# A token-mixing and MLP kernel: the input of batch 2 loaded in eight parts, each behind a product of batch 1

## The chip, the cores and the metric

The kernel runs on one core of a Trainium2 chip. The metric is the device time of one execution in microseconds (us), as the median of several runs. A core has five engines that run their own instruction streams and meet at semaphores: TensorE (PE, matrix products; its weight loads are listed as PEld), VectorE (DVE), ScalarE (ACT), GpSimd (POOL) and SyncE (SP). Transfers between the memory of the chip (HBM) and the core's own memory (SBUF) are done by 16 DMA engines. Any of SyncE, ScalarE and GpSimd can issue them. TensorE writes its results to a small memory of eight banks (PSUM), from which VectorE or ScalarE copy them out.

## The reference

There are two steps. The first mixes the 3008 tokens of each of 8 batches: a Fourier transform along the sequence, a product with a complex filter, and the transform back. The second is an MLP with an exact GELU on each of the 24064 tokens.

```python
def _attn_ref(x, filt_r, filt_i):            # x: (8, 3008, 256)
    X = np.fft.rfft(x, axis=1)
    F = (filt_r + 1j * filt_i)[None, :, :]   # filters: (1505, 256)
    Y = X * F
    return np.fft.irfft(Y, n=x.shape[1], axis=1).astype(np.float32)

def _moe_ref(x, w_in, w_out):                # x: (24064, 256), w_in: (256, 2048), w_out: (2048, 256)
    h = x @ w_in
    g = 0.5 * h * (1.0 + erf(h / sqrt(2)))
    return (g @ w_out).astype(np.float32)
```

## The kernel before

The transform of 3008 = 47 x 64 points is done as two shorter ones, each a matrix product with a table. For batch b there are stages `s1` (47-point products of the input x), `r1` (its result comes back through HBM in another order), `s2` (the second product, times the filter F on VectorE: twelve products p(0) to p(11), two frequencies each), `s3` and `r2` (the way back, again through HBM) and `s4`, which writes the mixed tokens y. Batch 0 has its own stages before the main loop. The MLP takes the tokens in 47 blocks of 512: `mm1` with GELU on ScalarE, then `mm2`. Block 0 does `mm2` plainly; from block 1 on it is done with seven products in place of eight, for which VectorE makes sums of the activations (`sums_1` to `sums_3`) and puts the results together (in `mm2_seven`).

The input of a batch is brought in by eight transfers, for 8 of 32 columns w and one of two halves h each. They convert fp32 to bf16 and are issued by GpSimd. There is one buffer x for all batches (pool `px`), so a load has to wait until `s1` of the batch before has read it.

```python
self.px = pool("px", 1)
self.pp = pool("pp", 6)      # the products p
self.po = pool("po", 4)      # output tiles, and the sums of mm2_seven, tag "ost"
...
def load_x(self, b, lo=0, n=32, hs=(0, 1)):
    ...
    for w in range(lo, lo + n, 8):
        for h in hs:
            nc.gpsimd.dma_start(out=xt[h * o:h * o + NA, w:w + 8, :], in_=xv[h][:, w:w + 8, :])

def gate(self, t):
    g = self.po.tile([1, 1], BF16, tag="gate", name="gate")
    self.nc.gpsimd.tensor_copy(out=g, in_=t)      # one element: GpSimd waits until t is written

def load_next(self, b, p, c, h):
    if b > 1:
        self.gate(self.st[b, "p", p][0:1, 0, 0:1])
    self.load_x(b + 1, 8 * c, 8, (h,))

def load_filters_again(self, eng, k0, k):         # F, now in another order of rows
    for o in range(0, 128, 32):
        i = self.st["Fd"][o // 64, :, :, :, k0:k0 + k, :].rearrange("q i t k c -> (q i) t (k c)")
        eng.dma_start(out=self.F[o:o + 32, :, k0:k0 + k, :], in_=i)
```

The gate makes GpSimd issue a load only once a given product p is there. It takes GpSimd alone; the value copied is used by nobody.

The work is spread by hand over slots: 16 slots are one block of 512 tokens in `mm1`, and the function `put` hangs a part of the mixing on a slot. What hangs on a slot is written into the program ahead of that slot's matmuls. For batch 1, `s2` of product p is at slot 28 + 14 * (p // 4) + 3 * (p % 4), which is 28, 31, 34, 37, 42, 45, 48, 51, 56, 59, 62, 65 for p = 0 to 11.

```python
for b in range(1, B):
    hi = first(b)
    if b == 1:
        s1, n1, r1, s2, n2, group = 0, 3, 12, 28, 3, 14
    elif b == 2:
        s1, n1, r1, s2, n2, group = hi - 87, 3.7, hi - 73, hi - 64, 3.4, 14      # hi = 176
    ...
    unit = lambda p: s2 + group * (p // 4) + int(n2 * (p % 4))
    ...
    if b + 1 < B:
        for i in range(8):
            put(unit(i + 2) if b > 1 else 25, m.load_next, b, i + 2, i // 2, i % 2)
...
put(4, m.table_4_all, parts[:5])                       # GpSimd
put(1, m.load_filters_again, nc.gpsimd, 0, 8)
put(17, m.load_filters_again, nc.sync, 8, 16)          # four transfers of 512 KB, on SyncE's queue
```

The output of the first blocks goes out on SyncE's queue too, that of later blocks on GpSimd's:

```python
# mm2 (block 0)
ost = self.po.tile([128, 2, 256], FP32, tag="ost", name="ost")
nc.vector.tensor_copy(out=ost, in_=ps)
for sub in range(2):
    self.put_rows(t * TCH + (tile_i - 1 + sub) * 128, ost[:, sub], nc.sync)
...
# mm2_seven: t1, t3 are the halves of one tile "ost" of sums; c(0, .) and c(1, .) are two more tiles, the results
v(out=c(1, 1), in0=t3, in1=p1, op=ALU.add)              # L688 of the trace
v(out=t1, in0=t1, in1=p1, op=ALU.add)                   # L691
...
v(out=c(h, 1 - h), in0=tt, in1=p, op=ALU.add)           # L694
self.put_rows(..., nc.gpsimd if t > 2 else nc.sync)
```

Of the kernel before, what the change touches and what calls it, by code (L numbers as in the profile page):

```python
# [31 lines left out]
class _Mix:  # L32
# [91 lines left out]

    def load_next(self, b, p, c, h):

        if b > 1:
            self.gate(self.st[b, "p", p][0:1, 0, 0:1])
        self.load_x(b + 1, 8 * c, 8, (h,))

# [603 lines left out]
def kernel(  # L734
# [9 lines left out]
    m = _Mix(ctx, tc, x, filt_r, filt_i, moe_w_in, moe_w_out, out)  # L744
# [115 lines left out]
    def put(slot, f, *a):  # L860
        at.setdefault(slot, []).append((f, a))

    def first(b):
        return (b * S // TCH) * 16

    busy, crowd, after = set(), set(), {}
# [5 lines that stand above are left out]
            s1, n1, r1, s2, n2, group = hi - 87, 3.7, hi - 73, hi - 64, 3.4, 14  # L872
        else:
            s1, n1, r1, s2, n2, group = hi - 94, 3.7, hi - 80, hi - 70, 3.4, 14
        unit = lambda p: s2 + group * (p // 4) + int(n2 * (p % 4))
        busy.update(range(s1 - 1, s1 + int(3 * n1) + 2))
        for c in range(4):
            put(s1 + int(c * n1), m.s1, b, c)
            put(r1 if c < 3 else unit(3) + 1, m.r1, b, c)
        for p in range(12):  # L880
            put(unit(p), m.s2, b, p)
            busy.add(unit(p))
            if p % 4 == 3:
                put(unit(p) + 3, m.s3, b, p // 4)
                put(unit(p) + 4, m.s3_out, b, p // 4, 1)
                busy.update(range(unit(p) + 2, unit(p) + 6))
        after[b] = unit(11) + 7
        crowd.update(range(s2, after[b]))
        if b + 1 < B:
            for i in range(8):  # L890
                put(unit(i + 2) if b > 1 else 25, m.load_next, b, i + 2, i // 2, i % 2)

    for b in range(1, B):
        end = 1000000
# [84 lines left out]
```

## Time and profile before

| what | before |
|---|---|
| time, median of 3 runs | 748.63 us (748.54 to 749.09) |
| span of the profiled execution | 747.3 us |
| TensorE busy | 736.0 us |
| VectorE, ScalarE, GpSimd busy | 573.2, 557.4, 224.8 us |
| DMA, mean over the span | 121 GB/s |

A line of the page's groups, or of an answer on one stretch of time, gives a program line (L688), an engine, the operation, and the tiles as "out<-in". A number in brackets is the time that the engine stood idle just before, with the event that ended it. In the chain of waits each row is a start, a length and what was going on; "SPq L113" is the queue of SyncE issuing the transfer of line 113 (the filters), and "DMA out_dram<-ost" is the time in which the store of an output tile was under way. In a table by stretches, each engine has its busy time and, in brackets, its number of instructions; the last columns are the clock granted to TensorE, the mean busy share of the 16 DMA engines (it is modelled, and a little over 1 when they are all full), and what they moved in GB/s. Of the DMA queues, q0 holds what GpSimd issues and q1 what SyncE issues; a row gives packets, MB, and the time that the packets took as a share of the stretch times 16 engines. L87 is the load of x, L113 the second load of the filters, L123 the gate, L430 a product p, L444 `s3`, L592 `mm1`, L595 the GELU, L665 `mm2` from block 1 on, L712 a store of the output.

### The profile page before, as it was taken

Reading aid. Unit: us, or ns where it says so; the run is one execution under the profiler, and the core shown is the slowest. Engines: PE = TensorE matmul, PEld = TensorE weight load, DVE = VectorE, ACT = ScalarE, POOL = GpSimd, SP = SyncE. Lnnn points to the kernel's source line nnn. Section 1 sums busy time; section 2 is a strip of 40 time slices with the busy share of each in tenths; the row PEclk is TensorE's granted clock in tenths of the full one; section 3 lists DMA queues with packets and bytes.
Section 4 is the critical chain, followed back from the end, with each engine's and each line's share of the span. In section 5 each row is a group of like instructions: output and inputs, shape, how many; then the busy total and the mean of one; then the engine's idle time right before and its main releaser. Section 6 shows DMA issues by size and latency. Waiting matters only on the chain.

```text
span 747.3 us, 20357 instructions
## 1 busy us (share of the span) xinstructions
PE 736.0 (98%) x8420; PEld 518.0 (69%) x8420; DVE 573.2 (77%) x1028; ACT 557.4 (75%) x1000; POOL 224.8 (30%) x416
## 2 busy tenths in 40 slices
PE   7999899999999999999999999999999999999998
PEld 4856566766777777677777776677677766777776
DVE  7876777787778887789767996779967798676566
ACT  6987677777787777777777777777778777777773
POOL 7994007142222413133311342114411121112121
PEclk9999999999999999999999999999999999999999
DMA  8999533666256651667426654256543533401011
GB/s 142 227 222 240 154 79 96 185 127 124 67 155 162 129 120 59 166 148 145 108 71 179 126 115 127 71 156 142 127 100 91 144 111 92 120 29 58 30 58 58
DMA packets 76663, 90.74 MB, mean 121 GB/s; under 512 B 9754, under 2 KB 57882, under 8 KB 76314
## 3 DMA queue, kind: packets, MB, share of 16 engines
q1 hardware_dynamic: 58714, 49.63, 26.1%
q0 software_dynamic: 17440, 39.62, 23.6%
q8 instruction: 66, 1.08, 0.6%
q14 instruction: 27, 0.22, 0.1%
q10 hardware_dynamic: 416, 0.20, 0.1%
HBM read 57.15 MB, written 48.23 MB: 141 GB/s over the span
## 4 chain that ended last, share of the span: by engine, by line
PE 86%; POOL 5%; DMA 5%; DVE 2%; issue 1%; ACT 1%; SPq 0%; POOLq 0%; DVEq 0%
PE ps_h L592 40%; PE ps_o L665 37%; PE ps_s L444 3%; PE ps_s L473 3%; DMA out_dram<-ost 2%; PE ps_s L427 2%; PE ps_s L400 2%; POOL tmp_sb L380 1%; POOL x_sb L87 1%; DMA F<-in_filt_i_dram 1%; DMA x_sb<-in_x_dram 1%; POOL F L118 1%; POOL T4a L382 1%; DVE g_sb L640 1%; DVE s_sb L634 1%
## 5 line engine op out<-in xcount | busy, mean ns | idle before, releaser
L595 ACT ACTIVATE g_sb<-ps_h 128x512 f16<-128x512 f32 x752 | 446.3, 600 | 169.6 <-PE ps_h L592 165.1
L592 PE MATMUL ps_h<-y_sb,w_in_sb 128*128 128x512 bf16 (+3 forms) x1600 | 445.0, 366 | 0.0
L712 POOL DMA_DIRECT2D out_dram<-ost x221 | 125.4, 574 | 430.4 <-DVE ost L694 410.5
L665 PEld LDWEIGHTS <-g_sb 128*128 128x128 f16 x2944 | 194.6, 98 | 80.1 <-issue 12.8
L665 PEld LDWEIGHTS <-s_sb 128*128 128x128 f16 x2208 | 148.7, 98 | 51.2 <-issue 5.8
L592 PEld LDWEIGHTS <-w_in_sb 128*128 128x128 bf16 x1600 | 125.0, 98 | 8.3 <-issue 1.7
L665 PE MATMUL ps_o<-w_sums,g_sb 128*128 128x128 f16 x1472 | 127.8, 219 | 1.3 <-DVE g_sb L640 1.1
L665 PE MATMUL ps_o<-w_sums,s_sb 128*128 128x128 f16 x1472 | 125.9, 219 | 0.0
L430 DVE TENSOR_TENSOR p<-ps_s,F 128x1024 bf16<-128x1024 f32 x84 | 102.4, 1219 | 26.9 <-PE ps_s L427 26.7
L634 DVE TENSOR_TENSOR s_sb<-g_sb 128x1024 f16<-128x1024 f16 x184 | 120.4, 683 | 1.0 <-ACT g_sb L595 1.0
L665 PE MATMUL ps_o<-w_out_sb,g_sb 128*128 128x128 f16 x1472 | 118.9, 219 | 1.8 <-DVE ost L694 1.7
L640 DVE TENSOR_TENSOR g_sb<-s_sb,g_sb 128x1024 f16<-128x1024 f16 x92 | 63.1, 686 | 1.1
L665 PE MATMUL ps_o<-w_out_sb,s_sb 128*128 128x128 f16 x736 | 63.8, 219 | 0.0
L647 DVE TENSOR_TENSOR s_sb<-g_sb 128x1024 f16<-128x1024 f16 x92 | 63.1, 685 | 0.0
L687 DVE TENSOR_TENSOR t_sb<-t_sb,ps_o 128x256 f32<-128x256 f32 x46 | 19.2, 418 | 46.5 <-PE ps_o L665 46.5
L473 PEld LDWEIGHTS <-d_sb 96*128 96x128 bf16 x448 | 31.9, 98 | 25.9 <-issue 0.2
L306 DVE CAST a_sb<-ps_s 128x512 bf16<-128x512 f32 x57 | 36.6, 686 | 15.1 <-PE ps_s L400 14.9
L682 DVE TENSOR_TENSOR ost<-t_sb,ps_o 128x256 f32<-128x256 f32 x46 | 19.2, 417 | 35.2 <-PE ps_o L665 34.9
L304 ACT ACTIVATE y_sb<-ps_s 128x376 bf16<-128x376 f32 x79 | 37.8, 479 | 2.6 <-PE ps_s L473 2.6
L694 DVE TENSOR_TENSOR ost<-t_sb,ps_o 128x256 f32<-128x256 f32 x90 | 33.6, 415 | 6.6 <-PE ps_o L665 6.2
L473 PE MATMUL ps_s<-T4a,d_sb 96*128 96x94 bf16 x448 | 38.1, 206 | 0.1
L123 POOL COPY gate<-p 1x1 bf16<-1x1 bf16 x40 | 13.8, 346 | 73.4 <-DVE p L430 73.4
(149 smaller groups left out, 529.3 us busy)
## 6 DMA issues: line engine op xcount, KB each, us to landing
out_dram<-ost POOLq DMA_DIRECT2D x123, 128.0 KB, 2.2
x_sb<-in_x_dram POOLq DMA_DIRECT2D x64, 188.0 KB, 4.1
b_sb<-R SPq DMA_DIRECT2D x28, 384.0 KB, 3.9
R<-v_sb SPq DMA_DIRECT2D x84, 128.0 KB, 2.4
d_sb<-R SPq DMA_DIRECT2D x56, 192.0 KB, 4.0
R<-a_sb SPq DMA_DIRECT2D x54, 192.0 KB, 3.1
F<-Fd SPq DMA_DIRECT2D x4, 512.0 KB
Fd<-F SPq DMA_DIRECT2D x8, 192.0 KB, 6.4
```

The costliest lines, as they stand in the source:

```text
L304: self.nc.scalar.activation(out=out, in_=in_, func=AF.Copy, scale=1.0 if scale is None else scale)
L306: self.nc.vector.tensor_copy(out=out, in_=in_)
L430: nc.vector.tensor_tensor(out=w, in0=ps.unsqueeze(1).to_broadcast([128, 2, 512]), in1=self.F[:, :, 2 * p:2 * p + 2, :].rearrange("p t a b ...
L473: nc.tensor.matmul(ps[:, 94 * i:94 * i + 94], lhsT=d[:, (grp % 2) * 4 + i, 128 * half:128 * half + 128], rhs=self.T4a[:, 4 * grp + i], sta ...
L592: nc.tensor.matmul(ps[:, o:o + n], lhsT=w[:, dc], rhs=self.ring[:, dc, off:off + n], start=(dc == 0), stop=(dc == 1))
L595: nc.scalar.activation(out=self.st["g", t][:, jc, :], in_=ps, func=AF.Gelu)
L634: self.nc.vector.tensor_tensor(out=self.st["s", t][:, i:i + 2], in0=a, in1=b, op=ALU.subtract)
L640: self.nc.vector.tensor_tensor(out=a21[:, k], in0=self.st["s", t][:, k, 0], in1=a22[:, k], op=ALU.add)
L647: self.nc.vector.tensor_tensor(out=self.st["s4", t][:, k], in0=a12[:, k], in1=s2[:, k], op=ALU.subtract)
L665: nc.tensor.matmul(ps[:, (m + 1) % 2, sub, :], lhsT=a[:, i, 128 * sub:128 * sub + 128], rhs=b[:, i], start=i == 0, stop=i == 7)
L694: v(out=c(h, 1 - h), in0=tt, in1=p, op=ALU.add)
L712: eng.dma_start(out=out, in_=tile_[lo - r0:lo - r0 + n])
```

## The change

The condition that left batch 1 out is taken away: the loads of batch 2's input, which all hung on slot 25 and had no gate, now hang on the slots of the products p(2) to p(9) of batch 1, each behind a gate on its product, as for all later batches. It is meant to spread the eight transfers over the stage in which batch 1 is mixed.

```diff
     def load_next(self, b, p, c, h):
 
-        if b > 1:
+        if b > 0:
             self.gate(self.st[b, "p", p][0:1, 0, 0:1])
         self.load_x(b + 1, 8 * c, 8, (h,))
 ...
         if b + 1 < B:
             for i in range(8):
-                put(unit(i + 2) if b > 1 else 25, m.load_next, b, i + 2, i // 2, i % 2)
+                put(unit(i + 2), m.load_next, b, i + 2, i // 2, i % 2)
```

## The prediction

> **What bounds the kernel now.** I began with the page. Its first lines say that TensorE is the engine to watch, and that its clock is at full speed everywhere (a row of nines), so a gain can only come from places where the matmul stream stops.
>
> ```profile
> PE 736.0 (98%) x8420; PEld 518.0 (69%) x8420; DVE 573.2 (77%) x1028; ACT 557.4 (75%) x1000; POOL 224.8 (30%) x416
> ```
>
> The span is 747.3 us, so TensorE is idle for about 11 us in all. Next I asked for busy time by stretches, to see where. From 120 to 720 us it is idle for only 0.35 us in total, so nothing that changes there can matter. The rest of the idle time lies in the start, in the last 10 us, and in one hole near 80 us. That hole falls in the stage which the change touches, so I cut the stage at the events that matter: the first load of batch 2's input (60.2 us), the time when the first changed load could start (67.4), and the hole itself (78.3 to 85.8).
>
> ```profile
> core 0: us, PE busy (x) PEld busy (x) DVE busy (x) ACT busy (x) POOL busy (x), PEclk, DMA share, GB/s
> 60.20:67.40 7.20, 7.20 (x69) 5.08 (x67) 6.80 (x10) 4.56 (x9) 4.14 (x9) 1.00 1.02 228
> 67.40:78.30 10.90, 10.90 (x122) 7.30 (x121) 5.57 (x10) 8.34 (x16) 0.00 (x0) 1.00 1.06 233
> 78.30:85.80 7.50, 5.41 (x53) 3.34 (x50) 7.42 (x13) 3.52 (x7) 0.00 (x0) 1.00 0.49 178
> 85.80:98.00 12.20, 12.19 (x136) 8.33 (x137) 10.06 (x16) 8.96 (x17) 0.00 (x0) 1.00 0.23 55
> ```
>
> The reader is to see three things. The DMA engines are full (share 1.02 to 1.06) for 18 us, and nearly empty afterwards. TensorE loses 7.50 - 5.41 = 2.09 us in the third row. And VectorE is full there (7.42 of 7.50), after a stretch in which it was half idle (5.57 of 10.90): it was held up and then caught up. The chain of waits names the holder:
>
> ```profile
> 58.93 0.59 SPq L113
> 59.53 0.04 issue
> 59.57 0.94 SPq L712
> 60.51 0.04 issue
> 60.56 17.66 DMA out_dram<-ost
> 78.22 0.03 issue
> 78.25 0.05 DVEq L688
> 78.30 0.04 issue
> 78.34 0.42 DVE ost L688
> ```
>
> The store of the first output tile is issued at 59.57 and lands at 78.22. VectorE wants that buffer again for the second tile of token block 1 (the pool "po" has 4 buffers with the tag "ost": two for block 0, the sums and the first result of block 1, and then round again). The timeline of VectorE and of TensorE shows the price:
>
> ```profile
> 78.34 0.42 DVE L688 TENSOR_TENSOR ost<-t_sb,ps_o 128x256 f32<-128x256 f32 x1 [3.15 <-DMA out_dram<-ost]
> ```
> ```profile
> 79.15 0.56 PE L665 MATMUL ps_o<-w_out_sb,g_sb 128*128 128x128 f16 x7 [0.18 <-DVE t_sb L691]
> ...
> 82.75 0.45 PE L665 MATMUL ps_o<-w_out_sb,g_sb 128*128 128x128 f16 x5 [1.67 <-DVE ost L694]
> ...
> 85.81 0.51 PE L665 MATMUL ps_o<-w_sums,g_sb 128*128 128x128 f16 x6 [0.26 <-DVE g_sb L640]
> ```
>
> VectorE stands 3.15 us on a DMA; TensorE then waits for PSUM banks and sums that VectorE is late with: 0.18 + 1.67 + 0.26 = 2.11 us, which is the loss of the row above.
>
> Last, the DMA view over 60.2 to 80.2 us says who fills the DMA engines:
>
> ```profile
> q1 hardware_dynamic: 1230, 3.31, 64.9%
> q0 software_dynamic: 512, 1.54, 38.8%
> ```
>
> Queue q0 is the GpSimd queue and holds only the eight input loads here (8 x 188 KB = 1.54 MB). They take 38.8% of 20 us = 7.76 us of all sixteen engines, 0.97 us each. In the same view they land 11.9 to 16.4 us after issue, against a median of 4.1 us over the whole kernel. Queue q1 is SyncE's: four loads of the remaining filters (512 KB each, issued 57.0 to 59.5), behind them the stores of the output.
>
> **What the Trainium skill says.** "DMA: Bandwidth & Descriptors", section "Issuing engines are not separate DMA queues": transfers started by ScalarE, SyncE or GpSimd run on the same 16 DMA engines and interleave. The trace agrees: the two shares add up to 1.04 and both kinds of transfer are slow at once. Its section "Queues, rings and completion order" says that each DMA engine alternates between the queues that have work, packet by packet, and takes one queue's descriptors in order. That fits a store which stands behind 2 MB of filters in its own queue and gets only part of the engines while x is in the other. "SBUF — State Buffer", section "SBUF: two separate sides", says that GpSimd and VectorE share a port pair under an exclusive lock, and that a GpSimd DMA can starve because its descriptors can't be written. In this trace I see little of it: the issue of an input load takes 507 to 722 ns in all 64 cases, and the 40 gate copies take 177 to 578 ns.
>
> **The change part by part.**
> (1) It moves the eight loads of batch 2. Before, all are put at slot 25; GpSimd gets to them at 60.22, after its work on the table T4a, and issues them in 4.12 us. After, load i stands behind the product p(i+2) of batch 1, at slots 34, 37, 42, 45, 48, 51, 56 and 59. The order of instructions on TensorE, VectorE, ScalarE and SyncE stays as it is; only GpSimd's differs. From the end of the VectorE products in the trace the loads would go out at about 67.4, 69.5, 74.9, then near 78, 80, 82, 90 and 92 us (the last five estimated: today's 80.8 and later, less up to the 3 us that VectorE no longer stands).
> (2) It adds eight gate copies on GpSimd of about 0.25 us (median of the 40). GpSimd has nothing to do between 64.3 and 111.7 us, so their cost is nil. They read p, whose pool has six buffers, so eight VectorE products now also wait on GpSimd: p(8) for the gate on p(2), and so on. That gate is some 20 us old by then (67.4 against 89.9 us), and s3 reads p later than the gate does, so no buffer is held longer.
> (3) It frees the DMA engines from 60.2 to 67.4 us. The store needs the filters ahead of it and itself: of the 12.98 us that q1 took in this window (64.9% of 20 us) some 11 us come before the landing at 78.2, the rest being the second tile's stores and the first of R2. Alone it lands at about 60.2 + 11 = 71.2. Two of the eight loads get in before that, up to 2 x 0.97 us: 73.1 at the latest.
> (4) VectorE asks for the buffer at 75.19 (74.78 + 0.41, the end of L687). The store is there 2 us earlier. The wait of 3.15 us goes.
> (5) What then holds VectorE? L688 at 75.2, L691, L634; the product p(5) has its matmul at 76.3; two L634; L694 needs the last group of block 1 at 78.4. So L694 ends near 79.6, where TensorE asks for it at 81.0. The later L640 would end about 82.8, and TensorE would ask at 83.7. All three waits of TensorE go, with 0.9 us or more to spare.
> (6) The sum: -2.11 us. The 16 matmuls of s3 at 86.68 take 1.21 us instead of 0.99 as elsewhere, so 0.1 to 0.2 us more may lie there; I don't count it. Everything after is tied to the matmul stream and moves up as a whole. 748.63 - 2.11 = 746.5 us.
>
> **The rivals.**
> (a) The store stays late. If the filters and their neighbours alone take as long as I credit to both, it lands at 75 to 77 and VectorE still waits 1 us or so. TensorE has about 1 us of slack in that chain, so this would leave 0 to 0.8 us of the loss: 746.5 to 747.3. For it speaks that GB/s was 344 at the first moment of that window and mostly 200 to 260 afterwards, so the load is not simply shared by bytes.
> (b) A new collision takes the place of the old. The late loads (78 to 96 us) meet the stores of v_sb (issued 72 to 79 and 88 to 92) and the outputs of block 1 and 2. Against it: the DMA share there is 0.23 to 0.49, and six loads add 5.8 us of work over some 18 us, about a third. The chain that matters next, v_sb at 103.5 to d_sb landing at 112.1, begins after the last load has landed (92 + 4 = 96). It would give back at most the 0.5 us that TensorE waits at 114.3 today: 747.
> (c) The loads come too late for batch 2. Its first stage is put at slot 89, 119.8 us in the trace; with 20 us to spare this is out.
> (d) The gates or the descriptors get in VectorE's way through the shared port: eight times some 0.3 us on VectorE in a stage where it is 90% busy. Later batches run the same pattern with TensorE idle for 0.35 us in 150 us between 155 and 305 at the most, so I give it little: 746.7 to 747.
> (e) The transfers were hidden anyway, and the gain is eaten by a later wait. From 120 us on TensorE has no gaps to take it up. 748.6.
>
> **Range and chances.** I put 65% on the whole gain within 0.3 us (746.2 to 746.9), some 20% on (a), (b) or (d) with part of it (to 747.7), 10% on no gain or worse, and 5% on more than 2.8 us. Runs differ by some 0.5 us (748.54 to 749.09). So 746.5 us, with a range of 745.9 to 747.7. Two per cent are 15 us: the whole hole is 2.1 us, and nothing in the change can cost 15 us, so I put 0.99 on within 2%.
>
> **What would show it.** In the profile after, the first store of ost should land before about 75 us, the loads of x in about 4 to 6 us each instead of 14, L688 should have no wait for a DMA, and TensorE should lose under 0.3 us from 75 to 90 us. The share of the DMA engines should be below 1 after some 70 us and about 0.4 to 0.7 from 80 to 95. The matmuls of the first stage of batch 2 should start about 2.1 us earlier than 119.8. I am wrong if L688 still waits, if a v_sb or d_sb transfer becomes the releaser of TensorE near 100 to 114 us, or if the span keeps its length although the hole is closed.

## The result, and the profile after

| | before | after |
|---|---|---|
| median, six runs each | 749.09 us (748.54 to 749.76) | 746.50 us (745.96 to 747.16) |
| ratio, with 95% interval | | 0.9966 (0.9954 to 0.9979) |
| span of the profiled execution | 747.3 us | 745.3 us |
| TensorE's share of the chain that ended last | 86% | 91% |

The change saves 2.6 us by the medians, 0.34%. In the table by stretches of the kernel after, with the same cuts as in the prediction, the hole is closed:

```profile
core 0: us, PE busy (x) PEld busy (x) DVE busy (x) ACT busy (x) POOL busy (x), PEclk, DMA share, GB/s
60.20:67.40 7.20, 7.15 (x65) 5.19 (x65) 6.34 (x9) 4.54 (x8) 1.09 (x2) 1.00 1.03 243
67.40:78.30 10.90, 10.79 (x120) 7.30 (x121) 8.65 (x14) 8.34 (x16) 2.88 (x6) 1.00 0.95 232
78.30:85.80 7.50, 7.39 (x84) 4.88 (x83) 7.21 (x12) 5.25 (x10) 2.70 (x6) 1.00 0.67 129
85.80:98.00 12.20, 12.10 (x135) 8.91 (x134) 9.91 (x16) 9.17 (x17) 1.86 (x5) 1.00 0.56 105
```

TensorE is busy for 7.39 us of the third stretch in place of 5.41, and VectorE has 8.65 us of work in the second in place of 5.57: nothing holds it up there. The DMA share, 1.06 and 0.49 before, is now 0.95 and 0.67. (The trace of after holds 8287 matmul records in place of 8420, 133 fewer, so TensorE is busier than its column says. From here on starts of instructions are compared.)

The timeline of VectorE shows L688 without a bracket, so VectorE did not stand idle before it:

```profile
75.62 0.41 DVE L687 TENSOR_TENSOR t_sb<-t_sb,ps_o 128x256 f32<-128x256 f32 x1
76.07 0.42 DVE L688 TENSOR_TENSOR ost<-t_sb,ps_o 128x256 f32<-128x256 f32 x1
76.40 0.42 DVE L691 TENSOR_TENSOR t_sb<-t_sb,ps_o 128x256 f32<-128x256 f32 x1
```

GpSimd's timeline shows what the gates do. Each copy waits for its product, and one load follows:

```profile
68.31 0.58 POOL L123 COPY gate<-p 1x1 bf16<-1x1 bf16 x1 [6.95 <-DVE p L430]
68.85 0.59 POOL L87 DMA_DIRECT2D x_sb<-in_x_dram  x1
70.37 0.57 POOL L123 COPY gate<-p 1x1 bf16<-1x1 bf16 x1 [0.93 <-DVE p L430]
70.89 0.55 POOL L87 DMA_DIRECT2D x_sb<-in_x_dram  x1
75.77 0.18 POOL L123 COPY gate<-p 1x1 bf16<-1x1 bf16 x1 [4.33 <-DVE p L430]
76.00 0.51 POOL L87 DMA_DIRECT2D x_sb<-in_x_dram  x1
```

The eight loads go out from 68.9 to 92.5 us and land in 3.4 to 6.5 us, not 11.9 to 16.4. In the DMA view over 60.2 to 80.2 us, queue q1, which carries the filters and the stores, gets a larger part of the engines:

```profile
q1 hardware_dynamic: 1448, 3.76, 74.3%
q0 software_dynamic: 192, 0.58, 16.3%
```

The first output tile (two transfers of 128 KB) has landed at about 72.7 us, where it was 78.2.

A clean measure needs landmarks that both kernels have. I take the start of the first s3 of batch 1 and the start of the first s1 of batch 2. A late start of the whole program does not enter this interval, and that matters: the profiled execution of after was 0.84 us late by its first s3 (71.416 us against 70.574), after a prologue with the same instructions. The interval is 119.80 - 70.57 = 49.23 us before and 117.86 - 71.42 = 46.44 us after: 2.79 us shorter.

### The profile page after: what moved, and what is told of

Same layout as the page of the kernel before. It is cut to its first block, busy times and chain, and to the rows that moved or that the text cites. A ratio compares the mean times of both kernels' runs of the same rounds, so it can differ in the third digit from the quotient of the medians.

```text
span 745.3 us, 20244 instructions
## 1 busy us (share of the span) xinstructions
PE 728.5 (98%) x8287; PEld 518.7 (70%) x8420; DVE 573.2 (77%) x1028; ACT 557.5 (75%) x1000; POOL 227.7 (31%) x424
## 4 chain that ended last, share of the span: by engine, by line
PE 91%; DVE 2%; issue 2%; ACT 2%; DMA 2%; POOL 1%; DVEq 0%; POOLq 0%
PE ps_h L592 39%; PE ps_o L665 39%; PE ps_s L473 3%; PE ps_s L427 3%; PE ps_s L444 3%; PE ps_s L400 2%; ACT g_sb L595 1%; DMA x_sb<-in_x_dram 1%; PE ps_o L606 1%; DMA F<-in_filt_i_dram 1%; DVE p L521 1%; PE ps_c3t L554 1%; PE ps_c L539 0%; POOL x_sb L87 0%; DVE g_sb L640 0%
## 5 line engine op out<-in xcount | busy, mean ns | idle before, releaser
L592 PE MATMUL ps_h<-y_sb,w_in_sb 128*128 128x512 bf16 (+3 forms) x1471 | 417.5, 365 | 1.0
L123 POOL COPY gate<-p 1x1 bf16<-1x1 bf16 x48 | 17.4, 363 | 96.8 <-DVE p L430 96.8
```

The costliest lines, as they stand in the source:

```text
L592: nc.tensor.matmul(ps[:, o:o + n], lhsT=w[:, dc], rhs=self.ring[:, dc, off:off + n], start=(dc == 0), stop=(dc == 1))
```

## The experiments

All intervals below are this one, from the profile of the run named; 46.44 us turned out to be its floor. A ratio is that of the times, to the kernel before run beside it. My theory was that the burst of loads keeps the DMA engines full, so that an output buffer comes free late and VectorE, then TensorE, stand on it.

**One part alone: the slots without the gates.**

```diff
-                put(unit(i + 2) if b > 1 else 25, m.load_next, ...)
+                put(unit(i + 2), m.load_next, ...)
```

> One part of the change alone: the loads of batch 2 hang on the later slots, without gates. My theory (what counts is when the loads enter the DMA engines, and only the gate can hold GpSimd back, which otherwise waits for nothing after 60 us): the loads still start at about 60.5 us, the first store still lands near 78, VectorE still waits about 3 us, and the time is that of the kernel before (ratio 0.999 to 1.001). Rival (the place in the program is what counts): the ratio of the whole change, 0.9966.

Measured: ratio 0.9999 (0.9988 to 1.001), interval 49.17 us, landings of 11.9 to 16.5 us for the loads. VectorE's timeline:

```profile
78.53 0.42 DVE L688 TENSOR_TENSOR ost<-t_sb,ps_o 128x256 f32<-128x256 f32 x1 [3.10 <-DMA out_dram<-ost]
```

It is the kernel before. A later slot alone delays nothing here, since GpSimd has nothing else to do; it is the gates that hold the loads back. (Gates without the later slots are not possible: at slot 25 no product of batch 1 is in the program yet.)

**Delayed but not spread: one gate on p(2), all eight loads behind it; and one gate on p(4).**

```diff
-        if b > 0:
+        if b > 1 or p == 2:                   # second kernel: c == h == 0, with p = 4
             self.gate(self.st[b, "p", p][0:1, 0, 0:1])
...
-                put(unit(i + 2), m.load_next, b, i + 2, ...)
+                put(unit(i + 2) if b > 1 else unit(2), m.load_next, b, i + 2, ...)
```

> The change with only one gate: all eight loads go out together behind p(2), at about 69 us, so they are delayed but not spread. Theory A (the delay past the filters is what counts): the first store lands by 75, no wait at L688, ratio 0.996 to 0.998. Theory B (the spreading is what counts): a burst of 7.8 us of DMA work at 69 us still holds the store back to 77 or later, or delays the next stores so that another wait appears; ratio above 0.9985. I lean to A with a rest of up to 1 us of waiting, since the store is at most 3 us from landing when the burst starts.

> The change with one gate, on p(4): all eight loads in one burst at about 75.5 us, after the first store has landed (71 to 73). The burst lies over the stores of v_sb and the second output tile in place of the filters. If only the filters and the first store matter: no waits, ratio as the change, 0.996 to 0.9975. If a burst does harm wherever it lies, so that spreading is worth something: a new wait for v_sb or an output buffer, ratio above 0.998.

Measured: p(2): ratio 0.9964 (0.9953 to 0.9975); p(4): 0.9974 (0.9964 to 0.9985). The interval is 46.44 us in both, to the hundredth that of the change, although the loads land in 7.7 to 11.3 us and 3.5 to 8.7 us. No wait for a transfer is left on VectorE in either. So the delay is the whole gain, and the spreading, for which the change was made, adds nothing that can be seen.

**The bound: no loads of batch 2 at all.** This kernel leaves the eight loads out and mixes batch 1's input again in their place.

```diff
+        if b == 1:
+            self.st[2, "x"] = self.st[1, "x"]
+            return
         self.load_x(b + 1, 8 * c, 8, (h,))
```

> The kernel before without the eight loads of batch 2 (it mixes batch 1's input a second time in their place). It leaves 1.54 MB of transfers out and gives the bound of what any placing of these loads can bring. If the change has made the loads free, as I think: the ratio of the change, 0.996 to 0.9975. If the spread loads still cost something (gates, port, shared DMA engines): lower than the change by 0.0007 or more. The first store should land at about 71.

Measured: ratio 0.9964 (0.9951 to 0.9978), interval 46.44 us. The change has made these loads free: gates, descriptors and shared engines cost nothing that shows. The first tile, with no load beside it, lands at about 71.4 us.

**More output buffers.** A first attempt took two more output buffers and gave one of three buffers a_sb for them.

```diff
-        self.pa = pool("pa", 3)
+        self.pa = pool("pa", 2)
-        self.po = pool("po", 4)
+        self.po = pool("po", 6)
```

> The kernel before with six buffers for output tiles in place of four (paid for with two in place of three buffers a_sb); the loads stay in a burst at 60 us. My theory (the whole loss comes through the one output buffer whose store is late): the store lands as late as before, near 78, but nobody waits for it, TensorE loses under 0.4 us between 75 and 90, and the ratio is 0.996 to 0.9975. Rival (the full DMA engines also delay other transfers which hold TensorE): the wait moves to another transfer or to a later tile and the ratio stays above 0.9985.

Measured: ratio 1.0104 (1.009 to 1.0119), because of how I paid. The timelines of VectorE and TensorE of that run:

```profile
52.35 1.89 DVE L306 CAST a_sb<-ps_s 128x512 bf16<-128x512 f32 x3 [9.38 <-DMA R<-a_sb]
```
```profile
53.09 1.01 PE L592 MATMUL ps_h<-y_sb,w_in_sb 128*128 128x512 bf16 x2 [8.17 <-DVE a_sb L306]
```

With two buffers, s1 of batch 1 waits for a store of a_sb, again a transfer in a full stretch (DMA share 1.02 from 36 to 53 us). The run says nothing on the output buffers. The second attempt took one more, paid for with one of the six buffers p:

```diff
-        self.pp = pool("pp", 6)
+        self.pp = pool("pp", 5)
-        self.po = pool("po", 4)
+        self.po = pool("po", 5)
```

> The kernel before with five output buffers in place of four and five buffers for the products p in place of six; loads in a burst as before. By the program, p(5) is written after s3 has read p(0), so five should do. If the whole loss comes through the reuse of that one buffer: the store lands near 78 as before, nobody waits, s3 of the second four products follows that of the first by 13.5 us in place of 16.1, ratio 0.996 to 0.9975. If the full DMA engines also hold TensorE in another way: 14 us or more and a ratio above 0.998.

Measured: ratio 0.9975 (0.9964 to 0.9987), interval 47.33 us. L688 no longer waits, though the tile lands 16.9 and 18.4 us after its two issues. But the profile of this execution has a wait that I had not seen:

```profile
74.56 1.23 DVE L430 TENSOR_TENSOR p<-ps_s,F 128x1024 bf16<-128x1024 f32 x1 [3.40 <-DMA F<-Fd]
```

p(4) waits for the filters, which land at 74.5 us. The answer on line 430 of the kernel before, for 69 to 77 us, has the same wait in VectorE's queue (count, then shortest, median and longest in ns, then first and last start):

```profile
L430 DVEq EVENT_SEMAPHORE  x2: 50/1514/2978, 70.4 to 70.5; - x2
```

The longer one began at 70.5 and lasted 2.98 us. I take it for the wait for the filters, since it shrinks to 0.70 us in after and to 0.26 us without the loads. It ended at 73.5 us, 0.1 us ahead of p(4) at 73.64, so it held nothing up. The burst was close to having a second victim.

**Is that the five buffers p, or scatter?**

> The kernel before once more, to see how much the filters' landing scatters between executions. They landed at 73.5 us in the first profile, 2.9 us after s3 of the first four products began, 0.1 us before p(4) could start. Within 0.3 us of that: the landing is steady and the buffers p changed it in the run with five output buffers. 1 us or more off: it is scatter.

> The kernel before with five buffers for the products p in place of six and nothing else: the price of what paid for the fifth output buffer. If that is nil: L688 waits about 3 us on the store, p(4) doesn't wait for the filters, s3 to the first stage of batch 2 takes 49.2 us as before, ratio 0.999 to 1.001. If five buffers p are what held p(4) in that run: p(4) is 1 us late here too.

> The kernel with five output buffers and five buffers p once more, beside the two others. If the late filters (74.5 us, 4.3 us after s3 began) are a property of this program they are back, and s3 to the first stage of batch 2 takes 47.3 us again; if they were scatter, 46.4 to 46.6 us.

Measured: five buffers p alone, ratio 1.0004 (0.9991 to 1.0018), so they cost nothing, and p(4) is in time. The five output buffers once more: the wait for the filters ended 1.3 us after the first s3 in place of 4.2, p(4) was in time, and the interval is 46.44 us, the floor. In the kernel before once more it ended 1.5 us after the first s3 in place of 2.9. So the late filters were scatter. What I had not expected is that the first wait scatters as well. The kernel before, profiled again:

```profile
77.26 0.42 DVE L688 TENSOR_TENSOR ost<-t_sb,ps_o 128x256 f32<-128x256 f32 x1 [2.10 <-DMA out_dram<-ost]
```
```profile
81.67 0.45 PE L665 MATMUL ps_o<-w_out_sb,g_sb 128*128 128x128 f16 x5 [0.97 <-DVE ost L694]
84.72 0.51 PE L665 MATMUL ps_o<-w_sums,g_sb 128*128 128x128 f16 x6 [0.26 <-DVE g_sb L640]
```

The four profiled executions with four output buffers, the burst at 60 us and the stores where they were, beside those without a wait:

| run | wait at L688 | interval | above 46.44 |
|---|---|---|---|
| before | 3.15 | 49.23 | 2.79 |
| slots only | 3.10 | 49.17 | 2.73 |
| before, again | 2.10 | 48.17 | 1.73 |
| five buffers p | 1.43 | 47.50 | 1.06 |
| after; bursts on p(2), p(4); no loads; five output buffers, again; first tile by GpSimd (below) | 0 | 46.44 | 0 |

In the run with five buffers p the bracket names another store:

```profile
75.89 0.42 DVE L688 TENSOR_TENSOR ost<-t_sb,ps_o 128x256 f32<-128x256 f32 x1 [1.43 <-DMA R<-v_sb]
```

That store of v_sb was only issued at 75.78 us. The tile's own store landed at 75.77, and L688 began 0.12 us later, as in the kernel before (78.22 and 78.34), so I count it as the same wait.

The last column is the wait less 0.36 or 0.37 us in every row with a wait. This is the mechanism with its size: TensorE has 0.37 us of slack in this chain, and every further microsecond that VectorE stands costs one.

Most of the scatter of the wait lies in when the transfers were issued against VectorE's work, less in how long they took. Count from the issue of the last filter load. In the four rows with a wait, in their order, VectorE asked for the buffer 16.3, 16.6, 17.1 and 17.6 us after that issue, and the first tile landed 19.3, 19.6, 19.1 and 18.9 us after it. The landing moves by 0.7 us and the asking by 1.3. Without the burst at 60 us (after, the bursts on p(2) and p(4), no loads) the tile landed 13.2 to 13.3 us after the issue, at least 3.3 us before VectorE asked.

**Which of the two comes late: the filters behind the store.**

```diff
-    put(17, m.load_filters_again, nc.sync, 8, 16)
+    put(24, m.load_filters_again, nc.sync, 8, 16)
```

> The kernel before, burst at 60 us and all, but with the four filter loads issued on slot 24 in place of 17, so that the first store stands ahead of them in SyncE's queue. The first store should land within 6 us of its issue, and nobody waits for it. But the filters (2 MB) then share the DMA engines with the burst from 61 us on and land near 77 to 79, and p(4), which asks for them at 73.6 us, should wait some 3 to 5 us for them. If the full DMA engines are the cause and the store only the place where it shows, the loss stays or grows: ratio 0.999 to 1.003, with VectorE waiting on the filters. If the order in SyncE's queue is the cause alone: ratio 0.996 to 0.998.

Measured: ratio 0.9979 (0.9972 to 0.9986), interval 47.26 us. The chain of waits of this run:

```profile
59.72 0.59 SPq L113
60.31 0.04 issue
60.36 14.32 DMA F<-Fd
74.68 0.03 issue
```

The wait moved from the store to the filters, as expected, but was smaller: they landed at 74.7, not at 77 to 79, and p(4) began 1.15 us late, measured from s3 (4.22 us in place of 3.07). That costs 0.82 us, so nearly the same slack, 0.33 us, holds here.

**The store in the other queue, ahead of the burst.**

```diff
-                self.put_rows(t * TCH + (tile_i - 1 + sub) * 128, ost[:, sub], nc.sync)
+                self.put_rows(..., ost[:, sub], nc.gpsimd if tile_i < 2 else nc.sync)
```

> The kernel before with the first output tile stored from GpSimd's queue, ahead of the burst of loads there, in place of SyncE's queue behind the filters. The burst, the filters and the load of the DMA engines stay. If the store is late because it stands behind 2 MB in its queue while the engines are shared: it lands about 3 to 5 us after its issue at 60.2, nobody waits for it, ratio 0.996 to 0.998. If any transfer is late in this stretch because the engines are full: it lands after 10 us or more and some of the wait stays, ratio above 0.998. The second tile's store is still late in both cases and could hold the sums of block 2 at about 83 us for under 1 us.

Measured: ratio 0.9967 (0.9956 to 0.9979), interval 46.44 us, no wait at L688. But the store did not land in 3 to 5 us: 10.4 and 11.3 us after the two issues, with no unfinished transfer ahead of it in its queue. Its second half landed at 71.57 us, 0.2 us before the last filter load. GpSimd's queue as such is not slow: the page of the kernel before gives a median of 2.2 us for its 123 stores of 128 KB. GpSimd's timeline also shows a side effect:

```profile
60.80 3.09 POOL L87 DMA_DIRECT2D x_sb<-in_x_dram  x6
70.27 0.51 POOL L87 DMA_DIRECT2D x_sb<-in_x_dram  x1 [6.38 <-DMA out_dram<-ost]
71.85 0.51 POOL L87 DMA_DIRECT2D x_sb<-in_x_dram  x1 [1.07 <-DMA out_dram<-ost]
```

The last two loads waited for the two halves of the store, so the burst was six loads at first. The test is not clean, but it shows two things. The store need not stand behind 2 MB in its own queue to take 10 us or more. And ahead of the burst it landed 13.4 us after the issue of the last filter load, about as without a burst, though six loads were under way beside it.

## Why the prediction was right

**The time.** 746.5 us was predicted and 746.50 measured. That is closer than the working deserves. The base of the sum was 748.63 us; the kernel before measured 749.09 in the six runs. The saving was put at 2.11 us and is 2.6 by the medians; the two differences, of about 0.5 us each, cancel by luck.

**Steps (1) and (2).** The gates do what I said. From an estimate of 67.4 to 92 us, the loads went out at 68.9 to 92.5, of which 0.84 us is the late start of that execution. Eight more gates on GpSimd and eight more waits on VectorE cost nothing: the interval is that of the kernel without these loads.

**Step (3), the store.** I put its landing at 71.2 us alone and 73.1 at the latest; it is 71.4 without the loads and 72.7 in the change. The numbers held, the reason only in part. I had it take its time behind the filters in SyncE's queue; from the other queue, with nothing ahead of it, it took nearly as long (10.4 and 11.3 us, against 12.2 and 11.6 behind the filters without the loads). What is shown is that behind the filters it is late when the loads share the engines from 60 us on, and not when they come 8 us later. Why a store at the head of its queue takes 10 us stays open.

**Steps (4) and (5).** The wait at L688 went altogether, and with it all three waits of TensorE. But "0.9 us or more to spare" was too much, since it left out the product p(7): in after VectorE ends p(7) at 84.95 us, and the matmul of s3 that needs it starts at 85.36. Less 0.05 us from the end of one to the start of the other, this is the slack of 0.36 us.

**Step (6), the term that was mis-sized.** I took the loss as the sum of the brackets in TensorE's timeline, 0.18 + 1.67 + 0.26 = 2.11 us. By starts it is more. From the matmuls of p(6) to those of p(7) before took 83.47 - 78.59 = 4.88 us, against 82.12 - 79.43 = 2.69 after; from there to s3, 3.21 against 2.78; from s3 to p(8), 2.80 against 2.64. That makes 2.19 + 0.43 + 0.16 = 2.78 us. A bracket counts from the modelled end of the last matmul. In a running stream the next one starts before that end (in after, a group starts at 79.43 with a length of 0.38, and the next at 79.65), so each of the three stops loses some 0.17 us more than its bracket says, as an average: (2.19 + 0.43 - 2.11) / 3. The last 0.16 us are the slow s3 that I had seen (1.21 us) and not counted. (The other groups of 16 matmuls take 1.06 us in the same view, not 0.99.) It was a fourth wait for VectorE: in the trace of before one matmul of this s3 starts at 87.27 us, released by the end of p(7) at 87.22.

**The rivals.** (a) said that TensorE has about 1 us of slack; it has 0.37, and a rest of 1 us of waiting would have cost 0.6. It did not come about. (b) and (d) cost nothing, by the same comparison as above. (c) and (e) did not happen: from the third s3 to the first s1 of batch 2 it is 19.48 us in both kernels (100.32 to 119.80, and 98.38 to 117.86), so nothing is given back on the way there. From that s1 to the end of the span it is 627.47 and 627.45 us, so nothing is given back later either.

**What I missed.** The filters were almost late too, 0.1 us before they were needed. And the loss is not a constant: in four profiles, two of the kernel before and two of kernels with the same order of work, it was 1.06 to 2.79 us. I sized the gain from one profile, which happened to show the largest wait of the four. In these four the time from the first s1 of batch 2 to the end was 627.45 to 627.71 us, so their spans (745.1 to 747.4 us) differ by this interval and by the prologue. How much of the spread of the kernel before over 29 runs (746.73 to 750.27 us) comes from this race isn't settled: the prologue scatters too (the first s3 began between 69.85 and 71.42 us in the profiles with three buffers a_sb).

## What to carry to other kernels

When a bulk load has 50 us of time, don't let it start in the same microseconds as transfers that are needed in 15: hold its issue back with something that the issuing engine must wait for, since a later place in the program alone did nothing on GpSimd, which was idle (ratio 0.9999). Where a tile's reuse waits for its store, one more buffer takes the wait away, but another transfer in the same full stretch can be next in line, so thin the stretch first. Size a gain from the starts of the same instruction in both traces, and from more than one profile when a transfer and an engine race for the same moment.

## What the runs showed of the hardware

- With the DMA engines full (share 1.0 and more), two stores of 128 KB took 10.4 and 11.3 us with nothing ahead of them in GpSimd's queue, and 12.2 and 11.6 us behind 2 MB of filters in SyncE's, with no input loads about. The Trainium skill, "DMA: Bandwidth & Descriptors", section "Queues, rings and completion order", says that the write which marks a transfer as complete lands only after all earlier writes of that DMA engine, across its queues. It says so of transfers that SyncE or ScalarE issue. If it holds for GpSimd's as well, it would explain why a store with nothing ahead of it in its queue took nearly as long; no run here tells it from plain sharing.
- In this kernel VectorE's wait passes to TensorE one for one beyond 0.37 us, over a range of 1.4 to 3.2 us.
- Landings in the full stretch scatter between executions, those without the burst hardly. Counted from the issue of the last filter load, the first tile landed 18.6 to 20.0 us later in six executions with the burst at 60 us and the tile's store behind the filters, and the filters 13.9 to 15.5; without the burst the tile landed 13.2 to 13.3 us later in four. An interval of 46.44 us, without such a wait, repeats to 0.01 us over six programs.
